# Values loaded by the gpsimd queue with conversion to bf16, in place of a float32 load and a cast

## Chip, core and metric

The kernel runs on one core of a Trainium2 chip. The metric is the device time of one execution in microseconds (us). Three runs of the kernel before gave 230.29, 230.45 and 232.12 us; the median is 230.45.

## What is computed

Causal attention over 4 batches of 8 heads, 768 positions and 64 values per head, and then a two-layer network over the 3,072 tokens. Three of the heads ("retrieval") see all earlier positions; the other five ("stream") see the first 4 positions (the sink) and a window of the last 64.

```python
scores = q @ k^T / sqrt(64)                 # [4, 8, 768, 768]
keep = causal                               # retrieval heads 0, 2, 6
keep = causal & (pos_k < 4 | pos_q - pos_k < 64)   # the other heads
a = softmax(where(keep, scores, -1e9))
x = (a @ v) with heads side by side         # [3072, 512]
h = x @ w_in                                # [3072, 2048]
g = max(h, 0) + alpha * min(h, 0)
out = g @ w_out                             # [3072, 512]
```

Inputs and output are float32 in device memory. The kernel multiplies in bf16.

## The kernel before

**Segments.** The work on attention is cut into 16 segments, n = 0 to 15: batch n // 4, and in it one of the four pairs of heads (2,6), (1,5), (0,4), (3,7). Pair (2,6) has two retrieval heads, pair (0,4) one, the other two none. Within a segment `hh` is 0 or 1 for the head of the pair.

**The hand-written order.** One long string of names, `ORDER`, fixes the order in which the program is issued. Each name is one small function with its segment: `Lq5`, `Lk5` and `Lv5` load q, k and v of segment 5; `Cq5`, `Ck5.0` and `Cv5` cast them to bf16; `Tq5` and `Tk5` transpose by TensorE into a bank of PSUM and `tq5`, `tk5.0` copy from there; `S5.1.2` multiplies scores, `s5.1.2` takes the exponential on ScalarE, `m5.1.2` masks on VectorE; `A5.1` multiplies with v, `a5.1` divides by the sums; `X5` transposes the result for the network. `P1.6` multiplies with w_in (network step 1, token block 1), `p1.6` and `g1.6` make the two-slope function, `O1.0.3` is a quarter of the multiplication with w_out, `o1.0` copies it out and stores it. `wi3` and `wo3` load a part of w_in and of w_out. Each engine runs its own instructions in the order of this string; between engines semaphores hold. So what stands in front of an item on its engine, or on its DMA queue, is settled by the string.

**Queues.** Most loads are issued by SyncE (SP). The weights, most outputs and two small k loads are issued by GpSimd (POOL), on the gpsimd queue, which can convert on the way: w_in and w_out come as float32 and land as bf16 (L713, L717). At most eight DMAs of each kind are in flight: a new one waits for the landing of the one eight before it.

**Values.** `load_v` (L228) calls `load_rows` (L231), which puts float32 rows into one of four buffers `vf`. A retrieval head is one load of 128 rows by 6 tiles of 64 values. A stream head of segments 0 to 7 is laid out with a step of 124 rows and needs a second load of 24 rows for the seventh tile; from segment 8 on it is a load of 112 rows by 7 tiles and a small load that repeats the 4 sink rows in each tile. Then `cast_v` (L352) copies the buffer to bf16 into one of five tiles `vb`, whose 65th column is one; for segments 0 to 2, 4 and 5 on POOL, from 6 on on VectorE (string `CV`). For segment 3 `cast_v_head` (L347) does one head on each of the two. For stream heads of segments 0 to 7 `sinks` (L307) copies the four sink rows of tile 0 into the other tiles. `AV` (L543, matmuls at L560) then reads `vb`.

**Start.** Up to about 31 us the first batch's attention runs (segments 0 to 3), with the casts of q and k on POOL, VectorE and ScalarE; the last multiplications with v there are `A3.1` and `A3.0`, and `Cv3.1` (VectorE) and `Cv3.0` (POOL) come before them. From then on TensorE works on the network of one batch and the attention of the next in turn.

The names and lines that matter below: L210 and L213 q loads, L224 and L247 k loads, L247 and L249 v loads of segments 0 to 7, L240 to L243 v and k loads from segment 8, L312 sink copies, L321, L325 and L334 casts of q and k, L349 and L354 casts of v, L369 transposes, L560 output matmuls, L605 network step 1, L625 step 2, L635 outputs.

The softmax here doesn't subtract the row's maximum and nothing guards it: scores larger than these inputs give would overflow.

## Time and profile before

| | |
|---|---|
| median of three runs | 230.45 us |
| span of the profiled execution, first to last instruction | 230.0 us |
| granted TensorE clock | 1.000 |
| PE (matmuls) busy | 221.2 us, 96% |
| PEld (weight loads) busy | 136.7 us, 59% |
| DVE (VectorE) busy | 153.3 us, 67%, 396 instructions |
| ACT (ScalarE) busy | 139.1 us, 60% |
| POOL (GpSimd) busy | 47.1 us, 20%, 96 instructions |
| queue q1 (issued by SP) | 26.97 MB in 86,168 packets, 59.7% of 16 DMA engines |
| queue q0 (issued by POOL) | 8.93 MB in 5,792 packets, 17.3% |
| HBM | read 27.55 MB, written 6.29 MB |

PE is TensorE's multiplying side, PEld its weight loads. "Busy" leaves out waits, branches and the issue of DMAs by SP and ACT; on POOL the issue of a DMA counts as busy. The page's view by 40 slices gives the share of the 16 DMA engines that was busy; it is 90% or more in nearly all slices from 6 to 150 us, and 0 to 30% after that. The chain of waits follows the work that ended last back through what released it; in it an entry "DMA vf<-in_v_dram" is the time between the issue of a load and its landing. In the views of waits a row "A <- B: total, times, longest" says that A's engine sat idle until B.

Of DMA packets, the trace records queue, start, duration and size. Loads of w_in and w_out appear with the size that is written (1,024 bytes for 2,048 read).

### The profile page before, as it was taken

What the parts mean: (1) busy time and instruction counts of PE and PEld (TensorE: products, weight loads), DVE (VectorE), ACT (ScalarE), POOL (GpSimd) and SP (SyncE); (2) the same over time, 40 slices, a digit from 0 to 9 for tenths busy, and PEclk for the clock granted to TensorE, in tenths of its full rate; (3) what the DMA queues carried; (4) which work ended last, traced back from release to release, by engine and by line L of the source; (5) the groups of instructions that cost most, each with busy time, mean ns of one, the idle gap of its engine ahead of it and who ended that gap; (6) DMA issues with size and microseconds to landing.
All of it is one profiled execution on the core that took longest, in us unless ns stands there. A gap on an engine that the chain in (4) does not pass through costs nothing.

```text
span 230.0 us, 5212 instructions
## 1 busy us (share of the span) xinstructions
PE 221.2 (96%) x1974; PEld 136.7 (59%) x2002; DVE 153.3 (67%) x396; ACT 139.1 (60%) x280; POOL 47.1 (20%) x96
## 2 busy tenths in 40 slices
PE   7989889999999999999999999999999999999994
PEld 7777857555566655565466445556854555554553
DVE  5688768997647866999997349979990345545110
ACT  6679647999968567554864874498422333623232
POOL 6658758000430643000002100010000020000000
PEclk9999999999999999999999999999999999999999
DMA  6979999999999999899979999893310130110033
GB/s 197 299 184 279 246 250 218 231 212 180 209 234 158 230 220 238 157 216 183 184 139 186 211 249 183 163 197 61 62 36 0 48 137 1 46 48 1 0 137 137
DMA packets 92448, 36.62 MB, mean 159 GB/s; under 512 B 79472, under 2 KB 90632, under 8 KB 92424
## 3 DMA queue, kind: packets, MB, share of 16 engines
q1 hardware_dynamic: 86168, 26.97, 59.7%
q0 software_dynamic: 5792, 8.93, 17.3%
q10 hardware_dynamic: 464, 0.40, 0.5%
q8 instruction: 15, 0.25, 0.5%
q14 instruction: 9, 0.07, 0.1%
HBM read 27.55 MB, written 6.29 MB: 147 GB/s over the span
## 4 chain that ended last, share of the span: by engine, by line
PE 85%; DMA 10%; SPq 1%; issue 1%; DVE 1%; POOL 0%; ACT 0%; DVEq 0%
PE P L605 36%; PE P L625 34%; PE P L560 6%; DMA vf<-in_v_dram 5%; DMA kf<-in_k_dram 4%; PE P L434 4%; PE P L644 2%; PE P L427 1%; PE P L585 1%; PE P L369 1%; SPq L247 1%; DVE vb L312 0%; SPq L224 0%; SPq L210 0%; DVE vb L349 0%
## 5 line engine op out<-in xcount | busy, mean ns | idle before, releaser
L617 DVE SCALAR_TENSOR_TENSOR g<-neg,oma,P 128x512 bf16<-128x512 f32 (+1 forms) x128 | 72.9, 610 | 39.7 <-ACT neg L610 38.6
L605 PE MATMUL P<-xT,w_in_b 128*128 128x256 bf16 (+1 forms) x503 | 89.5, 325 | 0.4
L610 ACT ACTIVATE neg<-P 128x512 f32<-128x512 f32 x96 | 54.3, 608 | 52.2 <-PE P L605 43.4
L625 PE MATMUL P<-w_out_b,g 128*128 128x512 bf16 x349 | 84.3, 379 | 1.5 <-issue 0.6
L605 PEld LDWEIGHTS <-w_in_b 128*128 128x128 bf16 x512 | 48.7, 98 | 32.4 <-DVE g L617 0.4
L625 PEld LDWEIGHTS <-g 128*128 128x128 bf16 x368 | 34.5, 98 | 36.8 <-issue 1.3
L473 ACT ACTIVATE eR<-P 128x448 bf16<-128x448 f32 (+6 forms) x63 | 36.6, 621 | 13.6 <-PE P L434 5.1
L635 POOL DMA_DIRECT2D out_dram<-ot x18 | 9.9, 553 | 117.5 <-ACT ot L631 117.5
L571 DVE TENSOR_TENSOR xn<-P,rcp 128x448 bf16<-128x448 f32 (+1 forms) x32 | 19.5, 608 | 1.1
L631 ACT COPY ot<-P 128x512 f32<-128x512 f32 x23 | 13.2, 594 | 11.0 <-PE P L625 8.6
L527 ACT ACTIVATE eS<-P 128x384 bf16<-128x384 f32 (+1 forms) x25 | 13.5, 570 | 3.4 <-PE P L505 2.6
L521 ACT ACTIVATE eS<-P 128x352 bf16<-128x352 f32 x30 | 13.8, 490 | 1.5 <-PE P L427 1.0
L560 PE MATMUL P<-vb,eS 128*128 128x65 bf16 x260 | 11.3, 193 | 1.5 <-DVE vb L312 0.8
L417 PE MATMUL P<-qT,kT 128*128 128x192 bf16 (+13 forms) x68 | 11.5, 251 | 1.1 <-ACT eR L473 0.6
L560 PEld LDWEIGHTS <-eS 128*128 128x128 bf16 x260 | 10.2, 97 | 3.5 <-issue 1.9
L570 DVE RECIPROCAL rcp<-P 128x7 f32<-128x7 f32 (+1 forms) x32 | 6.3, 197 | 7.2 <-PE P L560 6.9
L536 DVE TENSOR_TENSOR eS<-eS,ms_near 128x352 bf16<-128x352 bf16 x30 | 9.4, 336 | 2.3 <-ACT eS L521 2.2
L434 PE MATMUL P<-qT,kT 64*128 64x176 bf16 (+17 forms) x172 | 10.9, 250 | 0.0
L560 PEld LDWEIGHTS <-eR 128*128 128x128 bf16 x276 | 9.6, 97 | 1.5
L434 PEld LDWEIGHTS <-kT 64*128 64x128 bf16 x172 | 6.8, 94 | 6.0 <-issue 5.7
L560 PE MATMUL P<-vb,eR 128*128 128x65 bf16 x276 | 10.1, 193 | 0.0
L483 DVE TENSOR_TENSOR eR<-eR,mr_near 128x128 bf16<-128x128 bf16 (+5 forms) x36 | 6.9, 225 | 4.3 <-ACT eR L473 4.3
(104 smaller groups left out, 183.7 us busy)
## 6 DMA issues: line engine op xcount, KB each, us to landing
out_dram<-ot POOLq DMA_DIRECT2D x18, 256.0 KB, 3.7
vf<-in_v_dram SPq DMA_DIRECT2D x22, 192.0 KB
kf<-in_k_dram SPq DMA_DIRECT2D x21, 192.0 KB
qf<-in_q_dram SPq DMA_DIRECT2D x18, 192.0 KB
qf<-in_q_dram SPq DMA_DIRECT2D x7, 384.0 KB
w_in_b<-in_moe_w_in_dram POOLq DMA_DIRECT2D x8, 256.0 KB, 9.5
w_out_b<-in_moe_w_out_dram POOLq DMA_DIRECT2D x4, 512.0 KB, 13.6
kf<-in_k_dram SPq DMA_DIRECT2D x9, 196.0 KB
```

What stands on the lines that cost most here:

```text
L417: nc.tensor.matmul(to, keys, queries, start=True, stop=stop)
L434: nc.tensor.matmul(to, keys[own], queries[own], start=True, stop=True)
L473: nc.scalar.activation(ebuf[n, hh][:, lo:hi].rearrange("p (x c) -> p x c", x=len(parts)), P[:, got[0]:got[0] + len(parts), 0:(hi - lo) // ...
L521: nc.scalar.activation(slots, sc[:, 0:352].rearrange("p (s c) -> p s c", c=176), AF.Exp, scale=scale)
L527: nc.scalar.activation(slots, sc.rearrange("p x (s c) -> p x s c", c=192), AF.Exp, scale=scale)
L560: nc.tensor.matmul(pav[:, i, :], e[:, o:o + 128], vv[:, j, hh, 0:D + 1], start=(m == 0), stop=(m == len(terms) - 1))
L571: nc.vector.tensor_tensor(xn[n][:, 0:nt, D * hh:D * hh + D], pav[:, :, 0:D], rcp.to_broadcast([128, nt, D]), op=ALU.mult)
L605: nc.tensor.matmul(psg[:, w * i:w * (i + 1)], w_in_b[:, c, 128 * fb:128 * (fb + 1)], xT[:, c, o:o + w], start=(x == 0), stop=(x == 3))
L610: nc.scalar.activation(neg[t, f], bank(held["P", t, f][0]), AF.Relu, scale=-1.0)
L617: nc.vector.scalar_tensor_tensor(g_buf[t % 2][:, fb, 0:w], neg[t, f][:, c], oma[:, fb:fb + 1], bank(got[0])[:, c], op0=ALU.mult, op1=ALU.add)
L625: nc.tensor.matmul(bank(held["O", t, s][0]), g_buf[t % 2][:, f, 128 * s:128 * (s + 1)], w_out_b[:, f, :], start=(f == 0), stop=(f == 15))
L631: nc.scalar.copy(ot, bank(got[0]))
```

## The change

`load_v` no longer calls `load_rows`: it issues the loads on the gpsimd queue, straight into the bf16 tile `vb`. The buffers `vf` and the casts are gone. A stream head of segments 0 to 7 is now one load of 128 rows by 7 tiles; in the seventh tile the rows past the 24th belong to the next head and meet masked-out weights. The sink copies stay, under the name `Cv`, for the segments with stream heads among 0 to 7, all on POOL. The names that fall away are taken out of `ORDER` (`vz0` to `vz3`, `Cv0`, `Cv4`, `Cv8` to `Cv15`; `Cv3.0` and `Cv3.1` become `Cv3` at the place of the latter), `vz` is new, and every other name keeps its place. `load_rows` stays for k.

```diff
-    vf = [stat.tile([128, 7, 2, 64], fp32, name=f"vf{i}") for i in range(NF)]
...
     def load_v(n):
-        load_rows(n, v, vf)
+        vv = vb[n % NV]
+        for hh, h in enumerate(heads(n)):
+            o = (n // 4 * H + h) * S * D
+            if n >= LAY and not RETR[h]:
+
+                end = o + 112 * NT * D > B * H * S * D
+                nt = NT - end
+                nc.gpsimd.dma_start(vv[NSINK:116, 0:nt, hh, 0:D], dram(v, o, [[D, 112], [112 * D, nt], [1, D]]))
+                if end:
+                    nc.gpsimd.dma_start(vv[NSINK:100, 6, hh, 0:D], dram(v, o + 672 * D, [[D, 96], [1, D]]))
+                nc.gpsimd.dma_start(vv[0:NSINK, :, hh, 0:D], dram(v, o, [[D, NSINK], [0, NT], [1, D]]))
+                continue
+            nt, step = (6, 128) if RETR[h] else (7, 124)
+            nc.gpsimd.dma_start(vv[:, 0:nt, hh, 0:D], dram(v, o, [[D, 128], [step * D, nt], [1, D]]))
...
-    def cast_v_head(n, hh):
-        vv = vb[n % NV]
-        cast_of("PV"[hh])(vv[:, :, hh, 0:D], vf[n % NF][:, :, hh, :])
-        sinks(n, vv.rearrange("p t h c -> p h t c"), [hh], (nc.gpsimd.tensor_copy, nc.vector.tensor_copy)[hh])
-
-    def cast_v(n):
-        vv = vb[n % NV]
-        cast_of(CV[n])(vv[:, :, :, 0:D], vf[n % NF])
-        sinks(n, vv.rearrange("p t h c -> p h t c"))
+    def sink_rows(n):
+        sinks(n, vb[n % NV].rearrange("p t h c -> p h t c"))
...
-    for i in range(NF):
-        fill(f"vz{i}", vf[i][:, 6, :, :], 0.0)
+    fill("vz", vb_all[:, 4, 6, :, 0:D], 0.0)
...
-        if n == 3:
-            for hh in range(2):
-                item(f"Cv{n}.{hh}", cast_v_head, n, hh)
-        else:
-            item(f"Cv{n}", cast_v, n)
+        if n < LAY and n % 4:
+            item(f"Cv{n}", sink_rows, n)
```

## The prediction

> **What bounds the kernel now.** I read the waits first, split at 31 us, the end of the first batch's attention start-up. The columns are the total of the wait, how often, and the longest; of the answers only TensorE's own rows are shown. After 31 us:

> ```profile
> engine line waited for: us in total, times, longest us
> ...
> PE P L625 <- issue: 0.6, 4, 0.2
> ```

> That is TensorE's only matmul wait of any size in 199 us: nothing that becomes faster after 31 us can show in the time. Before 31 us:

> ```profile
> PE P L708 <- DVE busy L294: 1.1, 1, 1.1
> PE P L560 <- DVE vb L312: 0.8, 1, 0.8
> ...
> PE P L560 <- DVE vb L349: 0.5, 1, 0.5
> ```

> The two waits of L560 (the output matmuls A3.1) are the only ones of this length after the first microsecond, and v causes both. The chain of waits in order of time (start, length, what) shows how v gets there:

> ```profile
> 15.13 5.14 DMA vf<-in_v_dram
> ...
> 20.28 7.32 DMA vf<-in_v_dram
> ...
> 27.69 0.60 DVE vb L349
> ...
> 28.31 1.05 DVE vb L312
> ...
> 29.40 0.50 PE P L560 x11
> ```

> So the last v load of the first batch (Lv3, issued by SP at 20.28) lands at 27.6, DVE casts it, DVE copies the sink rows, and A3.1 goes on at 29.40. From there TensorE runs to the end at 227.2 practically without a gap. **The time is this moment plus a fixed 200 us of matmuls**, so I price the change by when A3.1 can run. Then comes POOL's timeline (start, length, line, operation, idle before it and its releaser), since v moves there:

> ```profile
> 7.89 0.96 POOL L334 CAST g<-kf 128x384 bf16<-128x384 f32 x2 [1.40 <-DMA kf<-in_k_dram]
> ...
> 17.77 0.63 POOL L312 COPY vb<-vb 4x192 f32<-4x192 f32 x2
> 18.36 0.77 POOL L713 DMA_DIRECT2D w_in_b<-in_moe_w_in_dram  x1
> 19.12 0.83 POOL L321 CAST g<-qf 128x768 bf16<-128x768 f32 x1
> ...
> 23.82 0.61 POOL L713 DMA_DIRECT2D w_in_b<-in_moe_w_in_dram  x1
> 24.43 0.52 POOL L334 CAST natm<-kf 128x384 bf16<-128x384 f32 x1
> 26.38 0.56 POOL L349 CAST vb<-vf 128x448 bf16<-128x448 f32 x1 [1.44 <-DMA vf<-in_v_dram]
> ```

> POOL is 20% busy over the span but about 70% busy from 8 to 32 us (5.41+6.31+6.02 of 24 us), casting q and k for TensorE's transposes. Last, the table by stretches puts the DMA share at 0.92 in 8 to 16 us, 1.12 in 16 to 24, 1.18 in 24 to 32 and 1.07 from 60 to 150 (packets overlap, so about 1.2 is full). The start-up competes for DMA.

> **The change part by part.** TensorE's and ScalarE's instructions keep their order.

> Removed: 15 whole casts and two half casts (five on POOL at 0.93 and a half at 0.56 = 5.2 us; ten on DVE at 0.62 and a half at 0.58 = 6.8 us), one sink copy on DVE (1.04), four memsets against one. All DVE casts but the half one run after 31 us, where TensorE waits for nothing: worth nothing. The half cast and its sink copy were the last steps before A3.1; their 1.65 us go, but two sink copies on POOL (0.34 each) take their place. SP issues 82 DMAs where it issued 129, so q and k loads move forward, at most into the gap of 13 to 16 us, where the DMA packet records show a share of 0.5 to 0.75.

> Added: 43 DMA issues on POOL. Three rows of POOL give the issue: 128 descriptors 0.54 (out), 256 0.62 (w_in), 512 0.77 (w_out), a line of 0.6 ns each; so 0.92 for a head of 128x6 rows of 64 and 1.00 for 128x7. From both sides: 0.54 at the least, and 1.5 if the slope doubled. The ten small sink loads go by the k loads of the same form (0.65). Sum about 38 us, 33 net: POOL goes from 47 to some 80 us busy. Behind them on POOL stand the casts of q and k, the weight loads, the masks ns and nr, and the outputs; the sink copies (Cv) wait there for landings.

> Start-up, POOL's queue item by item. Ck1.1 ends at 8.37 as before. Lv0 (2x0.92) to 10.21; Ck1.0 10.69; Cq1 11.52; Lv1 (2x1.00) 13.52; Cq2 14.35; Ck2 15.31; Ck3.0 15.83; Lv2 (0.92+1.00) 17.75; Ck3.1 18.27. Already here the transposes Tq2, which TensorE ran at 12.2, wait for Cq2 until 14.35: 2.1 us, of which the short stalls up to 14.5 (0.3 and 0.2 each) give some back. Next: sinks Cv1 18.90, wi0 19.6, Cq3 20.4, wi1 21.07. Now POOL waits for Lv2 (second half issued at 16.75).

> A v load of this form on this queue isn't in the trace. Its landing after issue has two ends: 2.3 us (out in a quiet stage) and 7.1 us (the fastest w_in, in this very stage). I take 5.5: the DMA share of 1.1 to 1.2 is nearer the busy end, but SP's queue will hold less. So Lv2 at 22.25; sinks Cv2 22.6, Cq5 23.4, Ck4.1 23.9, wi2 24.5; only then Lv3, its second half issued at 25.5, where SP issued it by 20.28. It lands at 31.0, its two sink copies end at 31.7, and A3.1 goes on **2.3 us later** than at 29.40. This covers the 2.1 us of Tq2: both lie on the same path and the later one counts. With 2.3 for the landing, A3.1 runs when TensorE gets there, from 28.3 (1.1 earlier) to 30.4 (all of Tq2's delay kept); with 7.1 both waits grow (Lv2 23.85, Lv3 issued 27.1, landed 34.2, ready 34.9): 5.5 us later.

> Behind Cv3 stand wi3 to wi4, issued from 31.7 instead of 27.44. P1.6 needs wi3 at about 36.3 (33 matmuls after A3.1) plus the delay itself, and wi3 to wi4 find DMAs that SP's loads have left; cover about 1 us on each (the last, wi4, landed at 41.85 before for a need at about 42.7). I cost it at nothing; without this cover it is 1 to 3 us. From 38 us on Lv5, Lv4 and Lv6 stand ahead of wo3. Later v loads stand behind outputs: Lv15 and Lv14 follow o3.1 (150.18), so issued by about 156 against 154 by SP, for matmuls at 162.4 and 163.7; nothing. Five vb tiles replace four vf and five vb; the load of segment n waits for segment n-5's matmuls, which are done at every such place (Lv9 near 84, its A4 at 66.6).

> [...] The trace first: the out DMA issued at 87.03 lay inside DVE's cast of 86.92 to 87.55 and took 0.63 instead of 0.54; two w_in issues beside the cast of 27.69 took 0.61 and 0.62, like the others. So I add at most 0.09 per meeting, and hidden. [...] For the first packet, the trace has 1.1 us after issue where the chip is quiet and 3.1 for the first w_in at 18.36. [...]

> The sum: span 230.0 + 2.3 = 232.3. The median of the runs shown is 0.45 above the profiled span, which I keep: **232.8 us**.

> **The rivals.** (1) *v overtakes, not slower.* On its own queue v is served in turn with q and k instead of behind them; the casts go, and A3.1 goes on up to 1.1 us earlier. It decides if Lv3 is issued before about 25 and lands within 3 us. For it: SP's v3 waited 7.3 us in line, and four POOL casts go from this stage. Against: POOL issues Lv3 in order after Cv2, whose wait it can't skip. Time 230.45 - 1.1 = 229.35; if all of Tq2's delay stays, 231.4.
> (2) *Packets.* Small packets with conversion may cost more than 256 bytes unconverted: the trace has 23 ns mean, 18 median for those, and 98 for 2 KB converted against 87 for 2 KB plain, one eighth dearer. From 60 to 150 us the share 1.07 leaves 0.13 x 90 = 12 us of DMA time below 1.2; about 14,400 v packets on 16 engines eat that at 13 ns more each. At 40 ns (17 more) that is 15 us, 3 over, plus 2 to 4 more at the start: 236 to 240.
> (3) *Late w_out.* Six v loads (4,992 packets, 5.8 us at 18.6 ns alone, 11.6 if they alternate with SP's) come ahead of wo3, which landed at 56.50 for matmuls at 63.97. It decides above 7.5 + 2.3 = 9.8 us: then 1.8 more, some 234.6; alone nothing.

> **How the numbers follow.** Late Lv3 0.50, (1) 0.23, (2) 0.15, (3) 0.12. About 1% (2.3 us) is what a measurement can tell from no change. Half of the first case lies above that (0.25), with (3) 0.12 and (2) 0.15: slower 0.52. The rest of the first and nearly all of (1): same 0.43. Faster by 1% would need more than all the waits of L560: 0.05. The range goes from inside (1) to inside (2): 229.5 to 237.0; the likeliest case's own is 229.4 to 236.

> **What would show it.** The half cast and the waits on L349 gone; POOL over 30% busy; v loads of 0.9 to 1.0 us; Lv3 issued near 25 and ready near 31.7; after that no PE wait above 0.3 us. It is wrong if A3.1 runs before 29.4, if v packets take over 30 ns, or if TensorE waits for w_in, w_out or v after 33 us.

## The result and the profile after

The changed kernel takes **241.77 us** (median of four runs, 241.08 to 242.43) against 230.37 (four runs, 229.62 to 232.12): 1.048 times as long, 95% interval 1.043 to 1.054. Slower was forecast; 232.8 us and a range up to 237.0 were not enough. A run more than 1.5% above the fastest of its kernel, as one each was in runs 3, 4 and 8 below, is left out of the medians and ratios.

The page of the changed kernel, profiled in an execution of 241.08 us: busy time of TensorE and POOL, the slices (a digit is a tenth, a slice 6 us), and the queues:

```profile
span 239.4 us, 5201 instructions
...
POOL 7784659820004595920001071046000020000000
PEclk9999798899999999999999999999999999999999
DMA  6999599999993999999928999949111130000033
...
q1 hardware_dynamic: 60240, 20.50, 43.7%
q0 software_dynamic: 33600, 12.30, 41.1%
```

Two things are new: the granted clock is not full in the fifth, seventh and eighth slices (before it was 9 in all forty), and q0 holds 27,808 more packets. 26,280 of all packets on it are v in pieces of 128 bytes, which took 32 ns in the median; the 256-byte packets on SP's queue take 18 over the whole span.

TensorE's waits of the changed kernel (total, times, longest):

```profile
PE P L564 <- DMA vb<-in_v_dram: 2.4, 1, 2.4
PE P L609 <- DVE xT L594: 2.0, 1, 2.0
PE P L373 <- POOL g L332: 1.6, 3, 1.0
```

Before, the longest wait after the first microsecond was 0.8. The two waits for VectorE's copy of v are gone. The chain of waits in order of time shows the path (start, length, what):

```profile
15.69 10.22 DMA vb<-in_v_dram
...
25.97 0.34 POOL vb L323
26.31 0.77 POOL natq L332
27.07 0.45 POOL natm L345
27.53 0.57 POOL w_in_b L717
28.09 0.92 POOL vb L240
29.01 4.32 DMA vb<-in_v_dram
...
33.38 0.35 POOL vb L323
...
33.77 0.50 PE P L564 x11
...
35.99 3.58 DVE ms L673 x2
...
40.45 6.16 PE P L609 x36
```

Lv2 is issued at 15.69 and takes 10.2 us to land. POOL stands at its sink copy; the second half of Lv3 can be issued only at 29.01, and A3.1 runs at 33.77. Then VectorE's `ms` (the table of mask factors, two tensor_scalars and three small copies) takes 3.6 us; its tensor_scalars took 0.32 before. TensorE's 2,002 weight loads come in the same order in both kernels, so each can be set against itself:

| step | before, us | after, us | later by |
|---|---|---|---|
| Tq2 | 12.16 | 13.66 | 1.5 |
| Tq3 | 20.17 | 21.40 | 1.2 |
| A2.1 | 22.28 | 25.95 | 3.7 |
| A3.1 | 29.40 | 33.77 | 4.4 |
| P0.1.2 (needs xT, which stands behind ms) | 33.70 | 40.45 | 6.8 |
| 77 weight loads further | 44.46 | 52.84 | 8.4 |
| X5 | 80.51 | 89.55 | 9.0 |
| last one | 226.89 | 235.92 | 9.0 |

So some 4.4 us are lost up to A3.1 and 4.6 behind it, nearly all before 53 us. The 1.65 between P0.1.2 and 52.84 are no wait. The table by stretches, here with the stretches that the clock records give (length, then busy time of PE, PEld, DVE, ACT and POOL, the granted clock, the DMA share and GB/s), shows what they are:

```profile
26.75:30.17 3.42, 3.42 (x48) 3.34 (x45) 2.06 (x5) 1.11 (x2) 3.42 (x6) 0.50 0.43 45
40.41:43.82 3.41, 3.37 (x13) 1.78 (x13) 1.56 (x3) 1.20 (x2) 3.41 (x6) 0.50 1.08 165
```

Right behind each of the two long waits TensorE ran 3.41 us at half clock. The first stretch costs nothing of its own, since A3.1 waits for Lv3 to 33.77 anyway (run 6 shows that wait grow when this stretch goes); the second, 99% busy, costs half its length, 1.7.

### The profile page after: what moved, and what is told of

The parts are those of the page before. It is cut to its first block, busy times and chain, and to the rows that moved or that the text cites. A ratio compares the mean times of both kernels' runs of the same rounds, so it can differ in the third digit from the quotient of the medians.

```text
span 239.4 us, 5201 instructions
## 1 busy us (share of the span) xinstructions
PE 226.8 (95%) x2002; PEld 138.6 (58%) x2002; DVE 152.4 (64%) x381; ACT 139.4 (58%) x280; POOL 77.5 (32%) x134
## 4 chain that ended last, share of the span: by engine, by line
PE 80%; DMA 8%; POOL 5%; DVE 4%; SPq 1%; issue 1%; ACT 0%
PE P L609 35%; PE P L629 32%; DMA vb<-in_v_dram 6%; PE P L564 5%; PE P L438 4%; POOL vb L240 2%; DMA kf<-in_k_dram 2%; DVE ms L673 1%; PE P L648 1%; PE P L431 1%; DVE eS L538 1%; DVE xn L575 1%; POOL g L345 1%; PE P L589 1%; PE P L373 1%; POOL g L332 1%
## 5 line engine op out<-in xcount | busy, mean ns | idle before, releaser
L621 DVE SCALAR_TENSOR_TENSOR g<-neg,oma,P 128x512 bf16<-128x512 f32 (+1 forms) x128 | 73.2, 610 | 42.7 <-ACT neg L614 41.6
L609 PE MATMUL P<-xT,w_in_b 128*128 128x512 bf16 (+1 forms) x512 | 92.1, 330 | 2.0 <-DVE xT L594 2.0
L629 PE MATMUL P<-w_out_b,g 128*128 128x512 bf16 x368 | 87.6, 379 | 0.0
L609 PEld LDWEIGHTS <-w_in_b 128*128 128x128 bf16 x512 | 49.3, 99 | 35.6 <-issue 3.5
L639 POOL DMA_DIRECT2D out_dram<-ot x18 | 10.2, 567 | 102.1 <-ACT ot L635 96.4
L240 POOL DMA_DIRECT2D vb<-in_v_dram x22 | 19.7, 906 | 3.8 <-DMA w_out_b<-in_moe_w_out_dram 2.2
L564 PE MATMUL P<-vb,eS 128*128 128x65 bf16 x260 | 11.6, 195 | 3.0 <-DMA vb<-in_v_dram 2.4
L421 PE MATMUL P<-qT,kT 128*128 128x192 bf16 (+13 forms) x68 | 12.2, 260 | 0.6 <-ACT eR L477 0.6
L323 POOL COPY vb<-vb 4x192 f32<-4x192 f32 x10 | 3.4, 340 | 25.3 <-DMA vb<-in_v_dram 25.3
L564 PEld LDWEIGHTS <-eR 128*128 128x128 bf16 x276 | 10.1, 99 | 1.5
L564 PE MATMUL P<-vb,eR 128*128 128x65 bf16 x276 | 10.6, 196 | 0.0
```

The costliest lines, as they stand in the source:

```text
L240: nc.gpsimd.dma_start(vv[:, 0:nt, hh, 0:D], dram(v, o, [[D, 128], [step * D, nt], [1, D]]))
L564: nc.tensor.matmul(pav[:, i, :], e[:, o:o + 128], vv[:, j, hh, 0:D + 1], start=(m == 0), stop=(m == len(terms) - 1))
L609: nc.tensor.matmul(psg[:, w * i:w * (i + 1)], w_in_b[:, c, 128 * fb:128 * (fb + 1)], xT[:, c, o:o + w], start=(x == 0), stop=(x == 3))
L621: nc.vector.scalar_tensor_tensor(g_buf[t % 2][:, fb, 0:w], neg[t, f][:, c], oma[:, fb:fb + 1], bank(got[0])[:, c], op0=ALU.mult, op1=ALU.add)
L629: nc.tensor.matmul(bank(held["O", t, s][0]), g_buf[t % 2][:, f, 128 * s:128 * (s + 1)], w_out_b[:, f, :], start=(f == 0), stop=(f == 15))
```

## The experiments

Each run is compared with runs of the kernel before on the same chip at the same time; "ratio" is to them, with its 95% interval. Shifts are TensorE's, against the profile of before. Of the string `ORDER` only the words around a move are shown.

**1 and 2. Only the later loads; only the start.** `load_v` takes the new way for some segments and the old way, with its casts, for the others: 4 to 15 in the first run, 0 to 3 in the second.

```diff
     def load_v(n):
+        if n not in SW:
+            load_rows(n, v, vf)
+            return
...
```

> Segments 4 to 15 by the gpsimd queue, segments 0 to 3 loaded and cast as before. If the loss is made in the first 40 us (Lv2 late, POOL's queue, VectorE's ms held up, the clock halved after each stall): 230 to 231.5 us, no TensorE wait over 0.6 us after 31 us. If the dearer v packets (32 ns against 18) or the loads behind outputs bind over the whole run: half of the loss or more stays, 236 us or more.

> The opposite half: segments 0 to 3 by the gpsimd queue, 4 to 15 as before. Start-up theory: 239 to 241.5 us, with the stall before A2.1, the long ms and two stretches at half clock. Whole-run theory: under 235 us.

Measured: the start alone **240.01** (ratio 1.034, 1.026 to 1.041), 8.9 of the 11.4 us and as much as expected. In its profile, though, the stall stands one step earlier than in the changed kernel's: the second half of Lv1 landed 11.9 us after its issue, POOL stood at its sink copy Cv1 with the cast Cq3 behind it, and TensorE waited for Tq3, not at A2.1:

```profile
PE P L390 <- POOL g L339: 5.4, 3, 4.5
```

Which load comes last at the start differs between executions: in runs 3, 10 and 11 Lv1 was late too and landed 10 to 12 us after its issue.

But the later loads alone gave **237.09** (1.023, 1.016 to 1.030), which the theory of the start did not allow and its rival did. TensorE's waits of the run with the later loads:

```profile
PE P L646 <- DMA w_out_b<-in_moe_w_out_dram: 3.7, 1, 3.7
```

Up to 61 us it runs as before (shift -0.4); at O0.3.3 it waits for the last part of w_out, goes on at 67.2 (shift +3.4), loses another 2.7 in the 6.8 us at half clock from 65.96 on, and ends 6.1 late. This part, wo3, stands on POOL behind the six loads Lv5, Lv4 and Lv6: it was issued at 49.04 instead of 38.89 and then took 18.1 us to land, where it took 17.6 before. So its lateness is POOL's order, and not dear packets, as the rival had it. In the full change the start's delay of 8 us hides this: wo3 lands at 71.97, 0.4 us before its matmul.

**3. ms out of the way.** The changed kernel with the item `ms` moved behind `p0.11`, some 18 us later.

```diff
-wi5 ms P0.1.0
+wi5 P0.1.0
...
-p0.11 P1.10
+p0.11 ms P1.10
```

> The changed kernel with the one item ms (five small VectorE operations in SBUF) moved later in the order, behind p0.11, where POOL mostly waits. If POOL's running instructions hold VectorE's ms up: ms 0.3 us instead of 3.6, TensorE's wait of 2.0 before the network's first step gone and the second stretch at half clock with it (3.4 us at half speed, 1.7), so 3.7 less: 238 us. If ms is slow for another reason, or something else is late there: within 1 us of 241.8.

Measured **242.47** (1.046, 1.036 to 1.056): no gain. The wait for xT is gone, and others stand there instead:

```profile
PE P L373 <- POOL g L332: 3.8, 2, 2.8
PE P L564 <- DMA vb<-in_v_dram: 1.9, 1, 1.9
PE P L629 <- DMA w_out_b<-in_moe_w_out_dram: 1.4, 1, 1.4
```

Tq3 came 3.2 us late instead of 1.2 in this execution (POOL stood at Cv1, the sink copy of Lv1, ahead of the cast Cq3 that Tq3 needs), and with less delay at 40 us the late w_out shows at 72.7. Taking one wait away is worth only what the next leaves.

**4. The queue without the conversion.** The kernel before with all v loads on the gpsimd queue as float32 into `vf`, and all casts kept.

```diff
     def load_rows(n, src, bufs):
+        eng = nc.gpsimd if src is v else nc.sync
...
-                nc.sync.dma_start(
+                eng.dma_start(
```

> The kernel before with v's loads moved to the gpsimd queue, but float32 into vf and all casts kept. If the conversion makes a v packet dear: packets of 256 bytes at 18 to 19 ns median, Lv2 lands in about 6 us instead of 10, 236 to 240 us. If the software queue itself makes small packets dear: 30 ns or more, and 241 to 246 us, since POOL has its casts back as well.

Measured **247.25** (1.066, 1.058 to 1.074), above the 241 to 246 of the theory that the queue makes packets dear. But most rows of v are not dear here: unconverted, they are recorded in packets of 4,096 bytes, the size of 16 rows, at medians of 172 to 288 ns in the stages up to 60 us, 11 to 18 ns a row. The few rows that stayed single on this queue, 144 packets of 256 bytes from 96 us on, took 33 ns in the median. So what goes with the conversion is that every row is a packet of its own; that a converted packet is dearer than another single row on this queue is not shown. The loads of Lv1 and Lv2 landed 5.7 to 7.7 us after their issue where the converted ones took 7.2 to 10.2. Of the 14.8 us that TensorE ends late in this run, 7.2 are there at A3.1, behind a POOL that here issues the loads and also casts; but 4.9 come only after 80 us, where TensorE waits for transposes by DMA and runs one stretch at half clock, and their cause was not followed. Moving the loads to this queue costs 16 us; with the conversion, and without the casts that it saves, the cost is 11.4.

**5. w_out ahead of the loads.** Run 1 with `wo3` moved behind `wo2`, ahead of Lv5, Lv4 and Lv6.

```diff
-kfz0 P1.8 wo2 P0.9 Lv5
+kfz0 P1.8 wo2 wo3 P0.9 Lv5
...
-P0.12 s4.1.2 wo3 O0.1.0
+P0.12 s4.1.2 O0.1.0
```

> This is the run with the twelve later v loads on POOL's queue and the first four as before, with one thing more: the last w_out load (wo3) is issued right behind wo2, ahead of the six loads Lv5, Lv4 and Lv6 instead of behind them. Theory (late w_out): the 3.7 us wait of O0.3.3 goes, with it the 6.8 us at half clock, and no other wait takes its place: time 229.5 to 231.5 against 237.1 without the move, ratio 0.995 to 1.005. Rival (converted packets of 32 ns are too dear for the DMA engines from 45 to 150 us): q, k, v or w_in land late elsewhere, TensorE waits over 1 us in sum after 60 us, 233 to 236.

Measured **232.0** (ten runs; 1.006, 1.003 to 1.010). This is 0.5 us above the range of the theory and below the rival's. The profile, of the fastest of the ten, has no wait of TensorE above 0.5 us after the first microsecond, and the clock stays at 1.0. So in it 19,496 packets of 32 ns hold up nothing from 50 us to the end; the one harm of the twelve later loads that a profile shows was w_out. In the means 1.1 us remain, 0.7 in the span and 0.4 outside it (2.1 us against 1.7); this was not followed further.

**6. TensorE kept busy in the waits.** The changed kernel with 38 matmuls of the zero tile before A2.1 and 30 before P0.1.2.

```diff
+    def filler(n):
+        b = min((x for x in range(8) if age[x] >= 0), key=lambda x: age[x])
+        for i in range(n):
+            nc.tensor.matmul(bank(b)[:, 0:128], busy, busy, start=True, stop=True)
...
+    item("F0", filler, 38)
+    item("F1", filler, 30)
```

> The changed kernel with idle time of TensorE filled: 38 matmuls of the zero tile of the warm-up (about 2.1 us) just before A2.1, which waits 2.4 us for v, and 30 (about 1.7 us) before P0.1.2, which waits 2.0 us for xT. Nothing else changes; the filling is not used. Theory (a 3.41 us stretch with some 2 us of idle is followed by one at half clock): the granted clock is 1.0 up to the end. The first half-clock stretch lies ahead of A3.1, which waits for Lv3 at 33.8 anyway, so only the second returns time, 1.7 us: 239.7 to 240.6 against 241.8. Rival (the half clock is hidden behind other waits, or follows from something other than idle): 241 to 242.5, or half-clock stretches remain.

Measured **240.52** (1.040, 1.031 to 1.049). Both half-clock stretches are gone from where they were. One is new: the wait before A3.1, now at full clock and so longer (2.0 us), lay unfilled, and 34.06 to 37.47 ran at half clock, against the expectation of a full clock to the end. The time is 1.25 us below that of the changed kernel, with overlapping intervals, and one stretch has only taken the place of another; the place of the stretches shows that they follow TensorE's idle time, the time does not.

**7. Lv3 ahead of the wait.** The changed kernel with `Lv3` ahead of `Cv2`, the sink copy that waits for Lv2.

```diff
-m10.0.2 X0 wi1 s2.0.0 Cv2
+m10.0.2 X0 wi1 s2.0.0 Lv3 Cv2
...
-a1.0 Lv3 Ck4.0
+a1.0 Ck4.0
```

> The changed kernel with one move in POOL's order: the two loads Lv3 stand ahead of Cv2, the sink copy that waits for Lv2, instead of behind Cv2, Cq5, Ck4.1 and wi2. Theory (the delay of A3.1 is made by POOL's order: the loads of Lv3 stand behind a wait for Lv2): Lv3 is issued at 21.9 to 23.8 instead of 28.1 to 29.9, lands by 30, and A3.1 runs at 30.5 to 31.5 instead of 33.8; time 238 to 239.5 if ms is held up as before. Rival (the DMA engines are the limit: what is issued earlier only waits in line): Lv3 lands at 31.5 to 33.5 and Lv2 later than 25.9; time 241 to 242.5.

Measured **236.95** (1.024, 1.016 to 1.031), 4.8 us less than the change and also less than the 238 to 239.5 expected. The chain of this run:

```profile
22.52 6.66 DMA vb<-in_v_dram
...
29.22 0.34 POOL vb L323
```

Issued 6.5 us earlier, Lv3 lands 4.2 earlier; A3.1 runs at 30.79, and the profiled execution has no half-clock stretch at all. So some 3.0 of the 4.4 us of A3.1 were POOL's order (Lv2 itself landed 0.6 earlier in this execution, so it may be less), and the rival (DMA throughput) falls for them.

**8 and 9. POOL kept busy beside ms.** The kernel before with four memsets on POOL behind `wi4`; then with four loads in the form of the new v loads there. They write to staging tiles that are free then.

```diff
-tq5 wi4 tk5.0
+tq5 wi4 J0 J1 J2 J3 tk5.0
...
+    for i in range(4):
+        fill(f"J{i}", vf[i], 0.0, nc.gpsimd)
```

Run 9 has in place of the last two lines:

```diff
+    for i in range(4):
+        to = vf[i][:, 0:2].rearrange("p t h c -> p (t h c)").bitcast(bf16)[:, 0:448]
+        item(f"J{i}", nc.gpsimd.dma_start, to.rearrange("p (t c) -> p t c", c=D), dram(v, 0, [[D, 128], [124 * D, 7], [1, D]]))
```

> The kernel before with four memsets of 128x896 float32 (0.85 us each, 3.4 us) on POOL behind wi4, into the staging tiles vf which are free then, so that POOL is busy from 28.6 to 35 without a gap while VectorE runs ms at 31.5 (0.32 us for its two tensor_scalars, POOL idle from 31.5 to 34.1). [...] Rival (POOL's own work does not hold VectorE; in the changed kernel it was the loads): ms takes 0.3 to 0.6, time 230 to 231.5.

> The kernel before with four loads in the form of the new v loads (128x7 rows, converted to bf16, 0.9 to 1.0 us of POOL each) behind wi4, into free staging tiles, in the place of the four memsets of the run before; what they bring is not used. Question: does the issue of DMAs by itself hold VectorE's ms, which starts at 29 to 31.5? If any instruction of POOL holds it, ms takes 3 to 5 us as beside the memsets; if only memsets, copies and casts do and an issue lets it through, ms ends with the cast or memset ahead of the loads, in 0.3 to 1.2 us. The time also holds the 3,584 added packets of v and waits of w_out behind them, so it is not judged.

The two tensor_scalars of `ms` on VectorE's timeline (start, length) in the profile of before:

```profile
31.53 0.32 DVE L669 TENSOR_SCALAR ms<-nms 128x192 bf16<-128x192 bf16 x2
```

What POOL did next there (idle before it and what ended it in brackets):

```profile
34.07 0.83 POOL L321 CAST natq<-qf 128x768 bf16<-128x768 f32 x1 [2.55 <-DMA qf<-in_q_dram]
```

The tensor_scalars in the changed kernel:

```profile
35.91 3.66 DVE L673 TENSOR_SCALAR ms<-nms 128x192 bf16<-128x192 bf16 x2
```

Beside the memsets, in run 8:

```profile
29.26 5.00 DVE L669 TENSOR_SCALAR ms<-nms 128x192 bf16<-128x192 bf16 x2
```

POOL's timeline of run 8 at this time:

```profile
28.70 0.63 POOL L713 DMA_DIRECT2D w_in_b<-in_moe_w_in_dram  x1
29.30 3.24 POOL L294 MEMSET vf<- 128x896 f32 x4
32.45 0.86 POOL L321 CAST natq<-qf 128x768 bf16<-128x768 f32 x1
33.21 0.93 POOL L294 MEMSET natk<- 128x960 f32 x1
34.05 0.79 POOL L717 DMA_DIRECT2D w_out_b<-in_moe_w_out_dram  x1
```

And beside the four loads, from run 9:

```profile
29.77 0.36 DVE L669 TENSOR_SCALAR ms<-nms 128x192 bf16<-128x192 bf16 x2
```

In run 8 four memsets, a cast and a memset that followed one another without a gap held the tensor_scalars 5.0 us, about the length of the row and not of one of the six (0.8 to 0.9), to the moment where POOL turned to the issue of w_out; TensorE waited 3.9 us for xT behind them. In the changed kernel POOL worked from 33.67 to 42.62 without a pause (from 35.97 on: a w_in issue, a memset, a cast, another issue, the cast Cq4, a memset, then w_out at 39.42), and `ms` ran from 35.91 to 39.57. Before, Cq4 waited for its load from 31.52 to 34.07, and `ms` fell into that pause. Times: memsets **236.8** (1.021, 1.013 to 1.030), above the author's estimate of 232 to 235.5 as well as the rival's 230 to 231.5; one run of the loads 235.73, in which TensorE waits 4.0 us for w_out, issued behind them as in run 1.

Run 9 does not answer its question: `ms` came at 29.77, between a cast (29.41 to 29.94) and the w_in issue behind it, and was nearly done when the first of the four loads was issued at 30.46. It shows that this w_in issue let VectorE in; the one at 37.21 in the changed kernel did not, and that at 35.97 only the first of the two tensor_scalars. The profile of run 11 bears on the question too: there the first tensor_scalar began at 18.30, inside the issue of Lv3's second half (18.04 to 18.97), and ended at 19.00, 0.70 us long where it took 0.20 before. So the issue of a v load held VectorE once. Which instructions of a row hold it and which let it in stays open.

**10 and 11. The repairs together.** The changed kernel with Lv3 as in run 7, wo3 as in run 5, and `ms` behind `X0`, where POOL pauses; in run 11 `Cq3` and `Lv3` stand even ahead of `Cv1`.

```diff
-X0 wi1 s2.0.0 Cv2
+X0 ms wi1 s2.0.0 Lv3 Cv2
...
-A0.0 Cv1 tq2
+A0.0 Cq3 Lv3 Cv1 tq2
```

> The changed kernel with three moves in the order: the loads Lv3 ahead of Cv2 (as in the run before), wo3 behind wo2, and ms behind X0, where POOL pauses for a landing. Theory (POOL's order, the hold-up of ms and the late w_out are what the change costs, apart from the late Lv2): against the run with Lv3 moved alone (236.95) the wait for xT goes (1.4 us) and no wait for w_out comes: 234 to 235.8; what is left above before is the wait for Lv2 and Tq2, 3 to 4 us. Rival (each repair only uncovers the next wait): 236 to 238.

> The run with the three moves, with one step more: the cast Cq3 and the two loads Lv3 stand ahead of Cv1, the sink copy that waits for Lv1, instead of behind it. Theory (what is left above before, 4.4 us, is POOL standing at a sink copy until a v load has landed, with work behind it that TensorE needs): Tq3's wait of 3.4 us goes; Lv3 is issued at 16.5 to 19 and lands by 28; A2.1 still waits 1 to 3 us for Lv2 itself, which lands near 25: 233 to 234.5. Rival (the early Lv3 only takes DMA time from Lv1 and Lv2, which land 1 to 3 us later): A2.1 waits 4 us or more, 235 to 237.

Measured **235.78** (1.020, 1.011 to 1.029) and **235.38** (1.022, 1.017 to 1.026). In run 10 `ms` takes 0.32 at 18.07 and w_out is in time; one long wait is left, and run 11 exchanges it for another. TensorE's longest wait in run 10:

```profile
PE P L373 <- POOL g L332: 4.1, 2, 3.4
```

In run 11:

```profile
PE P L564 <- DMA vb<-in_v_dram: 3.3, 1, 3.3
```

In the first, POOL stood at Cv1 until Lv1 landed (10.8 us after its issue) with Cq3 behind it; in the second Cq3 was in time, but Lv1 landed 11.8 and Lv2 10.8 us after issue. Its expectation is missed by 0.9 us: both theories hold in part, since the early Lv3 found its place (landed at 27.3) and the others came late. What is left is mostly the landing of the converted loads. No kernel of the study beats the one before.

## Why the prediction was wrong

**The landing of Lv2 was mis-sized.** The step took 5.5 us for a landing between 2.3 and 7.1; Lv2 took 10.2. (In runs 2, 3, 10 and 11 Lv1, of the same form, took as long.) The choice leaned on "SP's queue will hold less". By the packet records it does: 0.58, 0.92 and 0.45 of the engines in the three stretches of 4 us from 12 to 24 us, against 0.74, 1.06 and 0.74 before. But the gpsimd queue, which before had its first load issued at 18 us, adds 1.09, 0.41 and 1.08 to that, and both queues ran at once. The table by stretches, before:

```profile
12.00:16.00 4.00, 3.30 (x52) 2.78 (x51) 3.24 (x9) 3.83 (x6) 2.12 (x4) 1.00 0.74 154
20.00:24.00 4.00, 3.84 (x76) 3.56 (x75) 3.82 (x11) 3.38 (x5) 3.15 (x6) 1.00 1.18 242
```

and after:

```profile
12.00:16.00 4.00, 2.63 (x35) 2.05 (x33) 2.73 (x7) 3.39 (x6) 4.00 (x7) 1.00 1.69 260
20.00:24.00 4.00, 2.96 (x45) 2.40 (x43) 3.77 (x10) 3.69 (x6) 1.90 (x3) 1.00 1.55 221
```

The last two columns are the DMA share and GB/s: the share rises from 0.74 to 1.69 and from 1.18 to 1.55 (of a converted load the GB/s count what is written, half of what is read). "About 1.2 is full" was wrong too: the shares of two queues add up to more. So A3.1 came 4.4 us later instead of 2.3, inside the bound of 5.5 that the prediction had worked out. Its walk through POOL's queue held up to there: issues of 0.83 to 0.98 us (0.92 and 1.00 forecast), Lv2's second half issued at 15.7 (16.75), POOL 77.5 us busy (80). Lv3's second half came at 29.0 (25.5) only because of Lv2. Run 7 shows that this order is the larger part.

**"A fixed 200 us of matmuls after A3.1" failed**, and it carried the whole sum. Three things fell outside it: the row of POOL work that a late Cv3 pushed onto `ms` (2.4 us from A3.1 to P0.1.2), the half clock after waits (1.65), and X5 (0.65), which waited behind a masking step of VectorE that took 1.82 us beside POOL's mask work at 87 us, where the next took 0.35. The prediction had looked at the meeting of the two engines only from POOL's side, what a DMA issue loses beside VectorE (0.09), and never asked what VectorE loses beside POOL's casts and memsets. Of the clock it had said nothing, since before showed only 1.0.

**The base was off by 1.3.** The kernel's time lies 1.7 us above its span in 34 later runs of before (1.66 to 1.84 in nearly all), not 0.45, and their spans go from 227.5 to 232.1, median 229.3: the profiled execution was one of the longer ones. Its two waits for v before A3.1 were not typical either; with the same start, A3.1 ran at 27.00, 27.12, 27.64 and 28.88 in runs 5, 8, 9 and 1, against 29.40. So there was less to win than one profile showed, and against those four the changed kernel's A3.1 is 4.9 to 6.8 us late, not 4.4. Two smaller readings were off, with nothing resting on them: a third wait of 0.5 us (L417) stands beside the two of L560, and SP issues 156 DMAs before and 103 after, not 129 and 82. With the measured sizes the sum is 232.8 + 2.1 (A3.1) + 4.7 (behind it) + 1.25 (base) = 240.9, against 241.08 of the profiled execution.

**The rivals.** (1) did not occur, though two queues were served side by side in the profile of before (from 42 to 50 us 1,078 packets of q0 and 1,072 of q1 start). (2), dear packets: in the prediction's own terms, which are means, a packet of v took 33.2 ns against 23.2 for 256 bytes before. That is 10 more, not 17, and less than the 13 from which its estimate let them decide; from 60 to 150 us no profile shows a cost of them (run 5). At the start the converted loads land later than the unconverted ones (run 4). (3), late w_out, is real: in run 1 wo3 landed at 67.17 instead of 56.50, 10.7 us later, inside the 5.8 to 11.6 of the prediction and more than the 7.5 of slack. It cost 3.4 us, and another 2.7 at half clock, for which the prediction had no term. The way was another: not the packets ahead of it but its issue, 10.2 us later on POOL.

## What to carry to other kernels

A load moved to an engine that also computes is paid in that engine's order: list what stands behind each wait for its landing, price the landing by the fullest stage in the trace, and put issues ahead of waits (4.8 us here for one move, and 5 for moving w_out between runs 1 and 5). A fixed remainder behind a late step is an assumption: a delay moves other engines against each other, and what ran in a neighbour's pause may lose it (here the tensor_scalars of `ms`: 0.32 us before, 3.66 after). One profile of before is one draw; see how its waits differ between executions before counting them as a gain.

## What the runs showed of the hardware

**Converted rows were packets of their own.** In the changed kernel a row of 64 values converted on the way is recorded as a packet of 128 bytes and took 32 ns in the median (26,280 packets); unconverted on the same queue, the packets have the size of 16 rows, 4,096 bytes, and took 11 to 18 ns a row (run 4). Single unconverted rows of 256 bytes took 33 ns on that queue (144 packets of run 4) and on SP's queue 18 over the whole span, but 31 from 40 to 60 us in the changed kernel, beside converted loads. So no run shows that the conversion by itself makes a packet dearer. In the profiles of the seven kernels that load the first batch this way, Lv0 to Lv2 took 5.6 to 11.9 us to land.
